# Local and global attention, then two feed-forward layers: another order of TensorE's work in the attention loop

## The chip, the cores and the metric

The kernel runs on one core of a Trainium2 chip. The metric is device time in microseconds (us) of one execution, taken as the median of several runs. A profile is taken of one execution more; its span is the time from the first to the last instruction on the core. The engines work at the same time, each through its own list of instructions in the order in which the program issues them: TensorE (matrix products), VectorE (called DVE in the profile), ScalarE (ACT), GpSimd (POOL). SyncE (SP) issues the transfers between device memory and on-chip memory.

## The reference

Attention has 4 batches and 8 heads, 512 local tokens and 32 global tokens of dimension 64 per head. A global query attends to all 544 keys. A local query attends to the 32 global keys and to the local keys at most 32 positions away. Both results go through two feed-forward layers over 2304 tokens (512 wide, 2048 inside).

```python
def sm(s):
    s = s - np.max(s, axis=-1, keepdims=True)
    e = np.exp(s)
    return e / (np.sum(e, axis=-1, keepdims=True) + 1e-09)
k_all = np.concatenate([k_g, k_l], axis=2); v_all = ...          # the same for values
out_g = sm(scale * q_g @ k_all.T) @ v_all
mask = np.abs(pos[:, None] - pos[None, :]) <= 32
a_l = sm(concat(scale * q_l @ k_g.T, where(mask, scale * q_l @ k_l.T, -1e9)))
out_l = a_l @ concat(v_g, v_l)
x = concat(out_g, out_l)                                          # as (2304, 512)
h = np.maximum(x @ w1_in, 0);  x = (h * h) @ w1_out               # first layer
h = x @ w2_in;  out = (P(h) / (Q(h) + 1e-6)) @ w2_out             # second layer, P and Q polynomials
```

## The kernel before

Heads are worked two at a time: a pair p (16 of them, NP) is two heads on the 128 partitions, 64 each. The 512 local queries of a pair are cut in two units, (p, 0) and (p, 1), of 256 queries. The loop over p runs through 18 iterations; each holds pieces of several pairs, so that an engine always has something of another unit to do while one unit passes from engine to engine.

The pieces of a unit, with the letters that the change's name uses:

- **S**, `scores` (L311): 16 small products of 64x64 tiles into two PSUM banks, `s_ps[0]` and `s_ps[1]` for unit 0, `s_ps[2]` and `s_ps[3]` for unit 1. Each bank belongs to one head (j).
- VectorE's `maxima` (L320, two for each j) add the mask and take the row maximum; ScalarE's `exps` (L328, two for each j) take the exponential and its row sum; VectorE's `sums` and the reciprocal in `norm` (L332, L336) turn the sums round; GpSimd's four `norm` operations (L339) scale the weights.
- **T**, `transp` (L357 and L358): five 128x128 transposes into `tc_ps`. ScalarE copies four of them out (`transp_evac`, L362), VectorE the fifth (L364). GpSimd's `g_copies` (L350) add the weights of the global queries to the same tiles.
- **G**, `glob` in `pv` (L382): the products with the values of the global keys, 128x128 tiles. **W**, `win` (L376): the products with the values of the windows, 128x64 tiles; for unit 1 the last key columns follow (L396, called E here). VectorE copies the result into x (`pv_local` L403, `pv_global` L410 or L412).

The global queries of two pairs (2g and 2g+1) are worked together once every two iterations. **Q**, `g_scores` (L432, 128x64 tiles), writes into two PSUM banks, `s_ps[0]` and `s_ps[1]` (for g = 0 the banks of the value products); VectorE reduces them to a maximum (L435, L436, L441), ScalarE takes two exponentials straight from the banks (`g_exps`, L445, L446), VectorE and GpSimd normalise (`g_norm`, L450 to L452). **X**, `g_transp` (L461, L462), transposes the result into `s_ps[0]` and `s_ps[1]`, and ScalarE copies it out (L464, L465).

The order is written out by hand; no engine's instructions are reordered. In iteration p TensorE has S(p,0), T(p-1,0), G and W of (p-2,1), in odd iterations Q, then S(p,1), in even ones X, then T(p-1,1), G and W of (p-1,0). In the last two iterations, which have no scores, the first products of the feed-forward part (`mm1`) stand in their place.

Beside this the loop converts the first eight weight tiles of the feed-forward part, which arrive as 64-bit floats: ScalarE scales the upper word (`w_scale`, L94), VectorE puts the bits together in three steps (`w_float`, L106, L108, L113) and rounds (`w_split`, L124), GpSimd takes the rest (`w_rest`, L132). The list `slots` says in which iteration each tile is converted, here 6, 8, 10, 14, 16, 16, 17 and 17. In iterations 9 to 12 ScalarE also rounds the first 512 tokens of x (`x_high`, L156), in 10 to 13 VectorE takes their rest (`x_low`, L161). SyncE loads keys and queries of pair p+3 in iteration p, when the buffer of pair p-1 is free, values every second iteration, and weight tiles two iterations ahead of their conversion.

Behind the loop the memory of the attention part is freed, and the feed-forward part runs through steps s of `mm1`, `mm2` and elementwise work, with the other weight tiles loaded and converted on the way.

## Time and profile before

| | |
|---|---|
| time, median of 3 runs | 876.36 us (876.34 to 876.42) |
| the profiled execution | 876.76 us |
| its span | 875.0 us |
| TensorE busy (PE, matrix products) | 864.7 us, 99% of the span |
| VectorE busy (DVE) | 613.7 us, 70% |
| ScalarE busy (ACT) | 549.9 us, 63% |
| GpSimd busy (POOL) | 248.4 us, 28% |
| chain that ended last | PE 92%, DVE 2%, POOL 2%, ACT 1%, issue 1%, DMA 1% |

Busy time is the time in which an engine has at least one instruction under way. TensorE's instructions overlap, so its distance from one start to the next says more than its busy time. A start time in a row is counted from the beginning of the span. A note in brackets behind a row says how long the engine had been idle before and what it waited for.

### The profile page before, as it was taken

What the parts mean: (1) busy time and instruction counts of PE and PEld (TensorE: products, weight loads), DVE (VectorE), ACT (ScalarE), POOL (GpSimd) and SP (SyncE); (2) the same over time, 40 slices, a digit from 0 to 9 for tenths busy, and PEclk for the clock granted to TensorE, in tenths of its full rate; (3) what the DMA queues carried; (4) which work ended last, traced back from release to release, by engine and by line L of the source; (5) the groups of instructions that cost most, each with busy time, mean ns of one, the idle gap of its engine ahead of it and who ended that gap; (6) DMA issues with size and microseconds to landing.
All of it is one profiled execution on the core that took longest, in us unless ns stands there. A gap on an engine that the chain in (4) does not pass through costs nothing.

```text
span 875.0 us, 14523 instructions
## 1 busy us (share of the span) xinstructions
PE 864.7 (99%) x5335; PEld 771.4 (88%) x5335; DVE 613.7 (70%) x1353; ACT 549.9 (63%) x1175; POOL 248.4 (28%) x326
## 2 busy tenths in 40 slices
PE   8999999999999999999999999999999999999998
PEld 4877788888888999999999978888888999999998
DVE  5788888875554576552422599769777987987986
ACT  6888857773333333432445588668666876886885
POOL 4687754440000000000155342212221221221221
PEclk9999999999999999999999999999999999999999
DMA  9686549101553176140044200010001001001001
GB/s 347 261 329 242 212 166 410 75 1 48 169 145 109 46 220 199 47 139 1 25 110 132 73 13 1 0 49 1 1 0 49 1 1 37 1 1 37 1 1 37
DMA packets 27574, 81.67 MB, mean 93 GB/s; under 512 B 3184, under 2 KB 4976, under 8 KB 26480
## 3 DMA queue, kind: packets, MB, share of 16 engines
q1 hardware_dynamic: 27504, 80.76, 27.3%
q8 instruction: 42, 0.69, 0.3%
q14 instruction: 28, 0.23, 0.1%
HBM read 67.90 MB, written 12.85 MB: 92 GB/s over the span
## 4 chain that ended last, share of the span: by engine, by line
PE 92%; DVE 2%; POOL 2%; ACT 1%; issue 1%; DMA 1%; SPq 0%; POOLq 0%; ACTq 0%
PE tc L188 22%; PE pv L188 22%; PE s L175 14%; PE s L177 14%; PE s L176 14%; POOL sm L339 2%; PE pv L376 2%; PE tc L357 2%; PE s L311 1%; PE pv L382 1%; DMA k<-in_kW_dram 1%; PE s L432 1%; DVE sm L320 1%; ACT gs L445 0%; DVE tt L251 0%
## 5 line engine op out<-in xcount | busy, mean ns | idle before, releaser
L175 PE MATMUL s<-xh,w 128*128 128x384 f32 (+1 forms) x640 | 229.7, 359 | 0.0
L177 PE MATMUL s<-xh,w 128*128 128x384 f32 (+1 forms) x640 | 228.4, 357 | 0.0
L176 PE MATMUL s<-xl,w 128*128 128x384 f32 (+1 forms) x640 | 228.2, 357 | 0.0
L260 POOL TENSOR_TENSOR gl<-tt,gh 128x384 fp32r<-128x384 f32 (+1 forms) x79 | 90.1, 1140 | 267.9 <-ACT gh L259 205.2
L188 PE MATMUL tc<-gh,w 128*128 128x384 f32 (+1 forms) x640 | 152.8, 360 | 0.8 <-ACT gh L259 0.8
L188 PE MATMUL pv<-gh,w 128*128 128x384 f32 (+1 forms) x640 | 152.5, 360 | 0.0
L217 ACT ACTIVATE a<-s 128x384 f32<-128x384 f32 (+1 forms) x80 | 42.5, 532 | 152.5 <-PE s L177 152.5
L177 PEld LDWEIGHTS s<-xh,w 128*128 128x128 f32 x640 | 120.1, 188 | 11.4
L176 PEld LDWEIGHTS s<-xl,w 128*128 128x128 f32 x640 | 120.2, 188 | 10.8
L175 PEld LDWEIGHTS s<-xh,w 128*128 128x128 f32 x640 | 120.1, 188 | 10.5
L188 PEld LDWEIGHTS tc<-gh,w 128*128 128x128 f32 x640 | 115.9, 188 | 12.5 <-ACT gh L259 1.7
L188 PEld LDWEIGHTS pv<-gh,w 128*128 128x128 f32 x640 | 115.9, 188 | 11.8
L132 POOL TENSOR_TENSOR w<-raw,w 128x512 fp32r<-128x512 f32 x32 | 42.5, 1347 | 273.1 <-ACT w L126 263.3
L223 DVE TENSOR_TENSOR b<-a 128x384 f32<-128x384 f32 (+1 forms) x64 | 38.3, 599 | 116.2 <-ACT a L217 116.2
L188 PE MATMUL pv<-gl,w 128*128 128x384 f32 (+1 forms) x320 | 89.4, 360 | 0.0
L188 PE MATMUL tc<-gl,w 128*128 128x384 f32 (+1 forms) x320 | 89.2, 359 | 0.0
L237 DVE SCALAR_TENSOR_TENSOR a<-a,nf,b 128x384 f32<-128x384 f32 (+1 forms) x80 | 53.4, 668 | 32.2 <-ACT b L235 32.1
L234 ACT ACTIVATE a<-s 128x384 f32<-128x384 f32 (+1 forms) x80 | 42.0, 525 | 52.7 <-PE s L177 52.7
L339 POOL TENSOR_SCALAR sm<-sm,rs 128x160 f32<-128x160 f32 x128 | 57.1, 471 | 30.3 <-DVE x L410 12.3
L250 DVE SCALAR_TENSOR_TENSOR a<-a,b 128x384 f32<-128x384 f32 (+1 forms) x80 | 49.0, 612 | 22.0 <-ACT b L245 22.0
L188 PEld LDWEIGHTS tc<-gl,w 128*128 128x128 f32 x320 | 58.7, 188 | 6.0
L188 PEld LDWEIGHTS pv<-gl,w 128*128 128x128 f32 x320 | 58.7, 188 | 5.8
(117 smaller groups left out, 1342.4 us busy)
## 6 DMA issues: line engine op xcount, KB each, us to landing
v<-in_v_dram SPq DMA_DIRECT2D x8, 1408.0 KB, 8.3
k<-in_kW_dram SPq DMA_DIRECT2D x15, 592.0 KB, 6.4
r<-in_w1i_dram SPq DMA_DIRECT2D x16, 512.0 KB, 9.5
r<-in_w1o_dram SPq DMA_DIRECT2D x16, 512.0 KB, 10.3
raw<-in_w2i_dram SPq DMA_DIRECT2D x16, 512.0 KB, 4.2
st<-cv SPq DMA_DIRECT2D x32, 256.0 KB, 4.4
raw<-in_w2o_dram SPq DMA_DIRECT2D x16, 512.0 KB, 4.2
raw<-st SPq DMA_DIRECT2D x32, 256.0 KB, 2.7
```

The source lines that it names most:

```text
L132: pool.tensor_tensor(w[:, 1], f, w[:, 0].bitcast(F32), op=ALU.subtract)
L175: pe.matmul(ph, wh, hi[:, kk, :n], start=(kk == 0), stop=False)
L176: pe.matmul(ph, wh, lo[:, kk, :n], start=False, stop=False)
L177: pe.matmul(ph, wl, hi[:, kk, :n], start=False, stop=(kk == KD - 1))
L188: pe.matmul(acc_bank[d][:, :n], w[:, half, 128 * d:128 * d + 128], src[:, :n], start=start, stop=stop)
L217: act.activation(a, ph, AF.Relu)
L223: dve.tensor_tensor(b, a, a, op=ALU.mult)
L234: act.activation(a, ph, AF.Square)
L237: dve.scalar_tensor_tensor(a, in0=a, scalar=nf[:, 5:6], in1=b, op0=ALU.mult, op1=ALU.add)
L250: dve.scalar_tensor_tensor(a, in0=a, scalar=EPS1, in1=b, op0=ALU.add, op1=ALU.mult)
L260: eng.tensor_tensor(gl, t, gh.bitcast(F32), op=ALU.subtract)
L339: pool.tensor_scalar(e, e, rs[:, k:k + 1], 1.0, op0=ALU.mult, op1=ALU.mult)
```

## The change

The pieces stay the same; their order, their lag and a few sizes change. A unit's value products now come an iteration later: in iteration p they are those of b = (p-3, 1) and c = (p-2, 0), and the transposes those of a = (p-1, 0) and d = (p-2, 1). So the loop has one iteration more, and a third `mm1` stands in it. TensorE's list in iteration p is S(p,0), T(a), G(b), in odd iterations Q, W(b), W(c), in even ones X, G(c), T(d), and from iteration 2 on S(p,1) at the end. Maxima and exps of unit (p,1) move to iteration p+1, its normalisation too. The accumulation of a bank begins with G for unit 1 and with W for unit 0. The two reductions of Q move from `g_scores` to `g_scale`, which stands behind the sums of unit (p,0). For the first global scores other places are named: g = 1 is written into `s_ps[2]` and `s_ps[3]`, its exps and transposes stand in iteration 2. The first three weight tiles are converted in iterations 8, 10 and 12 instead of 6, 8 and 10; the first two VectorE steps of a tile stand at the end of its iteration, the third and the rounding at the end of the next one (the last four tiles are done whole). Buffers for values, softmax weights and their transposes grow in number.

```diff
--- before.py
+++ after.py
@@ -264,11 +264,11 @@
     msk_p = att.enter_context(tc.tile_pool(name="msk", bufs=1))
     ident = msk_p.tile([128, 128], F32, name="ident")
     mask = msk_p.tile([128, NB, KW], F32, name="mask")
-    v_p = att.enter_context(tc.tile_pool(name="v", bufs=2))
-    sm_p = att.enter_context(tc.tile_pool(name="sm", bufs=4))
-    pt_p = att.enter_context(tc.tile_pool(name="pt", bufs=3))
+    v_p = att.enter_context(tc.tile_pool(name="v", bufs=3))
+    sm_p = att.enter_context(tc.tile_pool(name="sm", bufs=6))
+    pt_p = att.enter_context(tc.tile_pool(name="pt", bufs=5))
     pg_p = att.enter_context(tc.tile_pool(name="pg", bufs=2))
-    st_p = att.enter_context(tc.tile_pool(name="st", bufs=4))
+    st_p = att.enter_context(tc.tile_pool(name="st", bufs=6))
 
     ff_p = {}
 
@@ -361,35 +361,28 @@
         p1, p2 = pT[p, u]
         act.copy(bass.AP(tensor=p1.tensor, offset=p1.offset, ap=[p1.ap[0], [320, 2], [192, 2], [1, 128]]),
                  tc_ps[0].rearrange("p (a b c) -> p a b c", a=2, b=2))
-        dve.tensor_copy(p2, tc_ps[1][:, 0:128])
-
-    def pv(p, u):
-
-        v = vt[p // 2]
-        c = pgT[p // 2][1]
-        p1, p2 = pT.pop((p, u))
-        bank = pv_ps[u]
-
-        def win(w, o0, o1, stop=False):
+
+    def transp_evac2(p, u):
+        dve.tensor_copy(pT[p, u][1], tc_ps[1][:, 0:128])
+
+
+
+    def pv_glob(p, u):
+        bank, v, p2 = pv_ps[u], vt[p // 2], pT[p, u][1]
+        for i in range(2):
+            o = VG + 256 * (p % 2) + 128 * i
+            pe.matmul(bank[:, 160 * i:160 * i + 128], v[:, o:o + 128], p2, start=bool(u) and i == 0,
+                      stop=not u and i == 1, skip_group_check=True)
+
+    def pv_win(p, u):
+        bank, v, p1 = pv_ps[u], vt[p // 2], pT[p, u][0]
+        for i, (o0, o1) in enumerate(((64, 160), (0, 64), (128, 224), (224, 288))):
             for j in range(2):
-                jj = 2 * (p % 2) + j
-                pe.matmul(bank[64 * j:64 * j + 64, o0:o1], v[:, VW * w + 64 * jj:VW * w + 64 * jj + 64],
-                          p1[:, j, o0 + (32 if o0 >= 128 else 0):o1 + (32 if o0 >= 128 else 0)],
-                          start=False, stop=stop, skip_group_check=True)
-
-        def glob(i):
-            o = VG + 256 * (p % 2) + 128 * i
-            pe.matmul(bank[:, 160 * i:160 * i + 128], v[:, o:o + 128], p2, start=i == 0, stop=False,
-                      skip_group_check=True)
-
-
-        glob(0)
-        glob(1)
-        win(4 * u, 64, 160)
-        win(4 * u + 1, 0, 64)
-        win(4 * u + 2, 128, 224)
-        win(4 * u + 3, 224, 288, stop=u == 0)
+                o, s = VW * (4 * u + i) + 64 * (2 * (p % 2) + j), 32 if o0 >= 128 else 0
+                pe.matmul(bank[64 * j:64 * j + 64, o0:o1], v[:, o:o + 64], p1[:, j, o0 + s:o1 + s],
+                          start=not u and i == 0, stop=False, skip_group_check=True)
         if u:
+            c = pgT[p // 2][1]
             for j in range(2):
                 jj = 2 * (p % 2) + j
                 o = VE + 64 * jj
@@ -418,7 +411,7 @@
     pg2 = [pg_p.tile([128, 128], F32, tag=f"pl{i}", name=f"pl{i}", bufs=1) for i in range(2)]
 
     def g_scores(g):
-        c1, c2 = s_ps[:2] if g else pv_ps
+        c1, c2 = s_ps[:2] if g > 1 else s_ps[2:] if g else pv_ps
         for c in (c1, c2):
             for i in range(2):
                 p = 2 * g + i
@@ -432,12 +425,12 @@
                 pe.matmul(c[o] if c is c1 else c[o, 0:64], qt[p][:, SL:], keys, start=True, stop=True,
                           tile_position=(0, 64 * i))
         m = st_p.tile([128, 8], F32, tag="gm", name="gm")
+        pgs[g] = pg[g % 2], m, c1, c2
+
+    def g_scale(g):
+        s, m, c1, c2 = pgs[g]
         dve.tensor_reduce(m[:, 0:1], c1[:, 32:], axis=AX.X, op=ALU.max)
         dve.tensor_reduce(m[:, 1:2], c2[:, 0:64], axis=AX.X, op=ALU.max)
-        pgs[g] = pg[g % 2], m, c1, c2
-
-    def g_scale(g):
-        s, m, c1, c2 = pgs[g]
         dve.tensor_scalar(m[:, 2:3], m[:, 0:1], m[:, 1:2], -0.125, op0=ALU.max, op1=ALU.mult)
 
     def g_exps(g):
@@ -503,12 +496,12 @@
 
         early = [(0, 0, j) for j in range(N_IN0)] + [(0, 1, j) for j in range(N_OUT0)]
         slots = {}
-        for p, c in zip([6, 8, 10, 14, 16, 16, 17, 17], early):
+        for p, c in zip([8, 10, 12, 14, 16, 16, 17, 17], early):
             slots.setdefault(p, []).append(c)
 
         for k in range(7):
             pe.matmul(pv_ps[0], warm[:, 0:128], warm, start=True, stop=True)
-        for p in range(NP + 2):
+        for p in range(NP + 3):
             if p == NP:
                 open_ff()
             if 1 <= p and p + 3 < NP:
@@ -521,99 +514,122 @@
                 w_load(*c)
             cv = slots.get(p, [])
             cur, pre = p < NP, 1 <= p <= NP
-            odd = p % 2 == 1 and p + 2 < NP
+
+            a = (p - 1, 0) if pre else None
+            b = (p - 3, 1) if 3 <= p else None
+            c = (p - 2, 0) if 2 <= p <= NP + 1 else None
+            d = (p - 2, 1) if 2 <= p <= NP + 1 else None
+            odd, even = p % 2 == 1 and 1 < p < NP - 2, p % 2 == 0 and 0 < p < NP
             g = (p + 1) // 2
 
-            def step(*k):
-                for c in cv:
-                    w_float(*c, k)
+
+            first = cv if p < NP else []
+            whole = cv if p >= NP else []
+            second = slots.get(p - 1, []) if p <= NP else []
 
             if cur:
                 sm_tiles(p, 0)
                 scores(p, 0)
+            elif p - NP < 3:
+                mm1(p - NP)
+            if pre and p > 2:
+                maxima(p - 1, 1, 0)
+                exps(p - 1, 1, 0)
+            if cur:
                 maxima(p, 0, 0)
                 exps(p, 0, 0)
-            else:
-                mm1(p - NP)
-            if 2 <= p:
-                pv_local(p - 2, 0)
-            if pre:
-                sums(p - 1, 1)
+            for n in (a, d):
+                if n:
+                    p_tiles(*n)
+                    if p > 1:
+                        g_copies(*n)
+            if a:
+                transp(*a)
+                transp_evac(*a)
             if cur:
                 maxima(p, 0, 1)
-            if pre:
-                norm(p - 1, 1)
-                p_tiles(p - 1, 0)
-                p_tiles(p - 1, 1)
-                if p > 1:
-                    g_copies(p - 1, 0)
-                    g_copies(p - 1, 1)
-            step(0)
-            if 2 <= p:
-                pv_global(p - 2, 0)
-            step(1)
-            if pre:
-                transp(p - 1, 0)
-                transp_evac(p - 1, 0)
-            step(2)
-            if cur:
                 exps(p, 0, 1)
-            if 2 <= p:
-                pv(p - 2, 1)
-            if odd and p > 1:
+            if p == 1:
+                g_norm(0)
+            if pre and p > 2:
+                maxima(p - 1, 1, 1)
+                exps(p - 1, 1, 1)
+            if a:
+                transp_evac2(*a)
+            if b:
+                pv_glob(*b)
+            if odd:
                 g_scores(g)
-            if cur:
+            if b:
+                pv_win(*b)
+            if c:
+                pv_win(*c)
+            if even and g > 1:
+                g_transp(g)
+            if c:
+                pv_glob(*c)
+            if b:
+                pv_local(*b)
+                pv_global(*b)
+            if d:
+                transp(*d)
+            if p < 2:
                 sm_tiles(p, 1)
                 if p == 0:
                     for k in range(4):
                         pe.matmul(pv_ps[0], warm[:, 0:128], warm, start=True, stop=True)
                 scores(p, 1)
-                if odd and p > 1:
-                    g_scale(g)
-                    g_exps(g)
-                maxima(p, 1, 0)
+                for j in range(2):
+                    maxima(p, 1, j)
+                    exps(p, 1, j)
+            if cur:
                 sums(p, 0)
                 norm(p, 0)
-                exps(p, 1, 0)
-                maxima(p, 1, 1)
-            if p == 1:
-                g_transp(0)
-                g_copies(0, 0)
-                g_copies(0, 1)
-                g_scores(g)
+            if odd or p == 2:
                 g_scale(g)
                 g_exps(g)
-            if odd:
+            if pre:
+                sums(p - 1, 1)
+                norm(p - 1, 1)
+            if c:
+                pv_local(*c)
+                pv_global(*c)
+            if d:
+                transp_evac(*d)
+                transp_evac2(*d)
+            if odd or p == 2:
                 g_norm(g)
-            for c in cv:
-                w_split(*c, dve)
-                w_rest(*c)
-            if p % 2 == 0 and 0 < p < NP:
+            for w in first:
+                w_float(*w, (0, 1))
+            for w in second:
+                w_float(*w, (2,))
+            for w in whole:
+                w_float(*w)
+            for w in second + whole:
+                w_split(*w, dve)
+                w_rest(*w)
+            if p == 2:
                 g_transp(g)
-            if 2 <= p:
-                pv_local(p - 2, 1)
-                pv_global(p - 2, 1)
-            if pre:
-                transp(p - 1, 1)
-                transp_evac(p - 1, 1)
-            if cur:
-                exps(p, 1, 1)
+            if cur and p > 1:
+                sm_tiles(p, 1)
+                scores(p, 1)
             if p == 0:
                 for k in range(4):
                     pe.matmul(pv_ps[0], warm[:, 0:128], warm, start=True, stop=True)
                 g_scores(0)
                 g_scale(0)
                 g_exps(0)
-                g_norm(0)
-            if pre:
-                pv(p - 1, 0)
-            for c in slots.get(p + 1, []):
-                w_scale(*c)
+            if p == 1:
+                g_transp(0)
+                g_copies(*a)
+                g_scores(1)
+            for w in slots.get(p + 1, []):
+                w_scale(*w)
             if 9 < p <= 9 + KD:
                 x_low(0, p - 10)
             if 9 <= p < 9 + KD:
                 x_high(0, p - 9)
-            if p >= NP:
+            if NP <= p:
                 ew1(p - NP)
         att.close()
         act.activation(nf[:, 0:4], cf[:, 0:4], AF.Copy, scale=-1.0)
@@ -644,7 +660,7 @@
         split = []
         made = []
         back = list(reversed(second))
-        used = [1, -1]
+        used = [2, -1]
 
         def load():
 
@@ -696,7 +712,7 @@
 
         load()
         magnitudes(2)
-        for s in range(2, 2 * S1):
+        for s in range(3, 2 * S1):
             t, j = divmod(s, KF)
             mm1(s)
             if j >= LAG:
```

## Rows read from the trace of the kernel before

**Rows 1.** Busy time of each engine by stretch: sum, instructions; then clock, DMA.

```profile
24.70:56.80 32.10, 31.52 (x468) 25.29 (x464) 24.24 (x147) 26.73 (x106) 21.13 (x53) 1.00 0.71 263
56.80:109.20 52.40, 50.62 (x737) 40.64 (x733) 44.22 (x243) 46.53 (x178) 40.57 (x89) 1.00 0.68 255
109.20:123.00 13.80, 13.80 (x117) 11.76 (x115) 10.55 (x27) 7.67 (x17) 7.55 (x10) 1.00 0.13 37
```

**Rows 2.** TensorE's timeline in pairs 11 and 12: start, duration, instruction, count.

```profile
82.72 0.78 PE L376 MATMUL pv<-p,v 128*64 128x96 f32 x16
83.43 0.77 PE L311 MATMUL s<-k,q 64*64 64x160 f32 x16
...
85.80 0.78 PE L376 MATMUL pv<-p,v 128*64 128x96 f32 x16
86.42 0.26 PE L396 MATMUL pv<-pl,v 128*64 128x32 f32 x4
```

**Rows 3.** The chain that ended last, same pairs: start, duration, what.

```profile
88.08 0.48 PE tc L357 x4
...
90.53 0.68 PE tc L357 x4
...
92.56 0.94 PE s L432 x4
```

**Rows 4.** VectorE's timeline in pair 1: start, duration, instruction, idle time before.

```profile
10.48 0.66 DVE L435 TENSOR_REDUCE gm<-pv 128x1 f32<-128x480 f32 x1 [1.93 <-PE pv L432]
...
11.30 0.21 DVE L441 TENSOR_SCALAR gm<-gm 128x1 f32<-128x1 f32 x1
12.69 0.21 DVE L450 TENSOR_SCALAR gm<-gm 128x1 f32<-128x1 f32 x1 [1.18 <-ACT gs L446]
...
13.02 0.31 DVE L320 CUSTOM_DVE_ANT_0 sm<-s,mask 128x160 f32<-128x160 f32 x1
...
15.69 0.21 DVE L332 TENSOR_SCALAR rs<-sum 128x4 f32<-128x4 f32 x1 [0.45 <-ACT sm L328]
15.93 0.18 DVE L336 RECIPROCAL rs<-rs 128x4 f32<-128x4 f32 x1
```

**Rows 5.** ScalarE's timeline in the same stretch.

```profile
11.61 0.66 ACT L445 ACTIVATE gs<-pv,gm 128x480 f32<-128x480 f32 x1 [2.25 <-PE tc L357]
...
12.27 0.30 ACT L446 ACTIVATE gs<-pv,gm 128x64 f32<-128x64 f32 x1
...
13.37 0.44 ACT L328 ACTIVATE sm<-sm,nm 128x160 f32<-128x160 f32 x1 [0.71 <-DVE nm L320]
...
14.23 0.57 ACT L362 COPY p<-tc 128x512 f32<-128x512 f32 x1
14.69 0.45 ACT L328 ACTIVATE sm<-sm,nm 128x160 f32<-128x160 f32 x1
...
16.41 0.56 ACT L464 COPY pg<-pv 128x512 f32<-128x512 f32 x1
```

**Rows 6.** VectorE's groups, pairs 8 to 15: count, busy us, mean ns, idle before.

```profile
L403 DVE COPY x<-pv 128x256 f32<-128x256 f32 x17 | 7.0, 414 | 0.0
...
L161 DVE TENSOR_TENSOR xl<-x,xh 128x512 fp32r<-128x512 f32 x4 | 3.2, 790 | 0.0
...
L108 DVE SCALAR_TENSOR_TENSOR cv<-r,cv 128x512 int32<-128x512 int32 x3 | 2.4, 788 | 0.0
L113 DVE SCALAR_TENSOR_TENSOR cv<-r,cv 128x512 int32<-128x512 int32 x3 | 2.1, 697 | 0.0
...
L124 DVE CAST w<-cv 128x512 fp32r<-128x512 f32 x3 | 1.6, 523 | 0.0
...
L106 DVE TENSOR_SCALAR cv<-cv 128x512 int32<-128x512 int32 x3 | 1.2, 394 | 0.0
```

**Rows 7.** GpSimd's timeline at the turn from pair 7 to pair 8.

```profile
56.18 1.56 POOL L339 TENSOR_SCALAR sm<-sm,rs 128x160 f32<-128x160 f32 x4 [1.04 <-ACT gs L445]
57.71 0.73 POOL L452 TENSOR_SCALAR gs<-gs,gm 128x544 f32<-128x544 f32 x1
```

More of the change, by code (lines that the diff above doesn't have):

```diff
@@ L434, in g_scores @@
         m = st_p.tile([128, 8], F32, tag="gm", name="gm")
-        dve.tensor_reduce(m[:, 0:1], c1[:, 32:], axis=AX.X, op=ALU.max)
-        dve.tensor_reduce(m[:, 1:2], c2[:, 0:64], axis=AX.X, op=ALU.max)
         pgs[g] = pg[g % 2], m, c1, c2
@@ L440, in g_scale @@
         s, m, c1, c2 = pgs[g]
+        dve.tensor_reduce(m[:, 0:1], c1[:, 32:], axis=AX.X, op=ALU.max)
+        dve.tensor_reduce(m[:, 1:2], c2[:, 0:64], axis=AX.X, op=ALU.max)
         dve.tensor_scalar(m[:, 2:3], m[:, 0:1], m[:, 1:2], -0.125, op0=ALU.max, op1=ALU.mult)
```

## The prediction

> **What bounds the kernel now.** I read the page first (TensorE is busy in nearly every slice), then the busy time by stretches [rows 1]. The three stretches are pairs 3 to 7, pairs 8 to 15, and the end of attention up to the fourth matmul group of the feed-forward part. Look there at TensorE against its stretch: 31.52 of 32.10 us, 50.62 of 52.40, 13.80 of 13.80. From 123.00 us to the end of the 875.0 us span the change touches nothing but the moment at which it starts, so I forecast that moment. The other engines are not idle either: in pairs 8 to 15 VectorE has 44.22 and ScalarE 46.53 us of work in 52.40. A pair takes 32.1/5 = 6.42 us in the first stretch and 52.4/8 = 6.55 in the second.
>
> Two views show what TensorE's time is made of. In its timeline, look at distances between starts: W takes 0.71 us when S follows (82.72 to 83.43) and 0.62 when E follows, which keeps the tile shape (85.80 to 86.42) [rows 2]. In the chain of waits T takes 0.68 us behind S and 0.48 behind X, the same shape [rows 3]. So changing the tile shape costs 0.1 to 0.2 us each time. Then I read the lists of VectorE and ScalarE in a stretch without conversions for the delay from one to the other [rows 4, 5]; both run strictly in the written order, and that decides my forecast.
>
> **Fewer changes of shape (gain).** Per pair TensorE now goes S-T-G-W-(E)-S-T-G-W-S: six changes. Afterwards it goes S-T-G-W-E-W-G-T-S-S: four (Q lies beside W and X beside G, free). Removed: two of W to S, at 0.10 on leaving and as I take it 0.05 in the first scores behind, 0.30; one of S to T, 0.20; one of G to W, for which I take 0.14 between the two. Added: W to G, which the trace does not show; I take 0.20 as for entering T, and T to S, 0.15 as for W to S. Net 0.64 - 0.35 = 0.29 us per pair. Each added one could cost from 0 to 0.3, so the net lies between 0 and 0.6 per pair, and only while TensorE is what is waited for.
>
> **Start (loss).** Up to Q of pairs 0 and 1 nothing changes. ScalarE ends their exponentials near 12.6 us [rows 5], and from then its list runs without a gap: a half-unit's two exps take 0.86 (14.69 to 16.41 holds two), a transposed copy 0.46. Up to the accumulated sums of unit (2,0) it has four such pairs and one copy of pair 1 and unit (0,0), the X copies (0.6), another pair, a copy, and a last pair with 1.00 to the VectorE sum (14.69 to 15.69 [rows 4]): 4x0.86 + 0.46 + 0.6 + 0.86 + 0.46 + 1.00 = 6.82, so 19.4 us. Only behind that sum does VectorE now reduce the scores of pairs 2 and 3: sum and reciprocal 0.34, reduce to scale 0.82, to the exp 0.31, between its two parts 0.66, to the norm 0.42, norm 0.33 [rows 4, 5]: 22.3 us. GpSimd meanwhile has two unit norms in its list ahead, 1.56 each from 19.9, so 23.0, then 0.73 for the global norm [rows 7]: 23.7. X of pairs 2 and 3 waits for it, and S(2,1) is written behind X: 0.7 each, so pair 3 starts at 25.1 instead of 24.70 [rows 1]: +0.4. TensorE idles some 3 us before X. What is not done by then (three pieces: two value products and a transposition, 3.3 us) comes back in the extra iteration at the end.
>
> **Iterations (the term that decides).** Let D be how long after the first scores of an iteration VectorE gets free of the last one's list. Its maxima of unit (p-1,1) come first; 0.35 later the exps start (13.02 to 13.37 [rows 4, 5]). ScalarE's order is fixed: pair, pair, copy, pair, and VectorE's sum of unit (p,0) stands behind the third pair: 0.35 + 0.86 + 0.86 + 0.46 + 1.00 = 3.53.
> In an odd iteration the global reduces now stand behind that sum: +0.34 + 0.82 + 0.31 + 0.66 + 0.30 = 5.96. These exps read the two banks that the next S(p+1,0) writes, so S waits: the iteration lasts at least D + 5.9. VectorE is free at 3.53 + 0.34 + 0.82 + 0.31 + 0.66 + 0.42 + 0.33 = D + 6.4.
> In an even iteration S(p+1,0) waits for the copy of X, behind the fourth pair: 0.35 + 4x0.86 + 0.46 + 0.56 = 4.81, at least D + 4.9 with the wait itself. VectorE is free at 3.39 + 1.00 + 0.34 + 0.6 (one 256-column copy, two short ones [rows 6]) = D + 5.35.
> So the excess handed on is 0.5 and 0.45 plus what else stands at the end of VectorE's list, and there the change puts the conversions of the early weights: L106 and L108 in even iterations 8, 10, 12, 14 (0.39 + 0.79, less 0.08 of overlap each as I take it: 1.05 rounded), L113 and L124 in the odd ones behind (0.70 + 0.52: 1.05), and in 10 to 13 the low part of x (0.79: I take 0.65) [rows 6]. Today they stand between waits.
> Without conversions D is about 0.5: TensorE's own work and the waits are about even, pairs 3 to 7 gain 5x0.29 = 1.45 (I let the waits of then and now, some 0.4 in an odd iteration, cancel).
> Pairs 8 to 15: p8 5.8 (TensorE's own work, some 5.6, and 0.2 for a weight scaling ahead of its exps on ScalarE); p9, D = 0.45 + 1.05 = 1.5: 7.4; p10, D = 0.5 + 1.05: 6.45; p11, D = 0.45 + 1.05 + 0.65 = 2.15: 8.05; p12, D = 2.2: 7.1; p13 8.05; p14 7.1; p15 has no Q and no gate: 6.42 - 0.29 - 0.94 [rows 3], 5.1. Sum 55.05 against 52.40: +2.65.
> Each gated iteration also pays semaphore instructions in front of waits; I take 0.1 in each of seven: +0.7 (from 0 to 0.2 each).
>
> **End.** The third feed-forward group now stands inside the attention loop. 13.8 us [rows 1] + 3.3 left from the start - 0.6 of saved changes: 16.5, so +2.7. Weights loaded into freed attention memory get one such group less of lead; the chain L106, L108, L113 (1.7 us at the most after the load [rows 6]) would show as a wait at the sixth group if the cover is gone; I price it at 0. More buffers: 0, memory alone. Keys of a pair are freed at the iteration's end instead of its middle; scores of two iterations later hide that load.
>
> **Sum.** 0.4 - 1.45 + 2.65 + 0.7 + 2.7 = +5.0 us. Against the profiled execution of 876.76 us this is 881.8; against the median of 876.36 it is **881.4 us**.
>
> **A rule that speaks against the change.** Granted clock is 1.00 in every stretch, where TensorE's idle time is 0.58 and 1.78 us in all [rows 1]. The Trainium skill ("TensorE: Matmul & The Clock Gate", "Why this matters for your kernels") warns that a long idle gap between bursts puts the array back to half rate; no row of this trace shows such a fall.
>
> **Rivals.** A, faster: the conversions sink into VectorE's waits, so TensorE stays the bound. Place: pairs 8 to 15; it decides if D stays under about 0.3 in odd and 0.7 in even iterations. Then they lose the 1.78 us of idle time and 8x0.29 = 2.3, -4.1, with no semaphore term: 0.4 - 1.45 - 4.1 + 2.7 = -2.45, 873.9 us. For it: VectorE has 8.2 us without work in that stretch. Against it: the written order, which lets nothing pass a sum that waits.
> B, about the same: iterations 8 to 15 stay as long as now, since VectorE's work is the same in amount: 0.4 - 1.45 + 2.7 = +1.65, 878.0. Against it: the two waits of VectorE per iteration (for the third and the fourth pair of exps) are new in place.
> C, slower still: the 3 us gap before X drops the array from 2.4 to 1.2 GHz, and one iteration's work of 6 us runs twice as long: +6 at the most, 887.4; +2 is nearer, as ScalarE has to be waited for there anyway: 883.4.
> D, the changes of shape cost nothing where the new order has them (the net gain per pair is 0): pairs 3 to 7 lose their 1.45 and the end its 0.6: +7.05, 883.4.
>
> **Chances.** Forecast 0.60, A 0.15, B 0.12, C 0.05, D 0.08. A difference under 0.2% (1.75 us) can't be told from none: faster 0.15, same 0.12, slower 0.73. The range takes in B, A's edge, C's and D's nearer values, and semaphore and shape terms at their ends: 873.5 to 886.0; the forecast's own range is 879 to 884.
>
> **What would show it.** TensorE idle about 3 us up to 23.7 before X (the transposes of the global weights); S(3,0) near 25.1. Then S(p+1,0) behind odd iterations waiting for ScalarE's L445 line, 0.4 us early on and 1 to 2 us from pair 9 to 13, behind even ones for the copy of X; iterations 9 to 14 of 6.4 to 8.1 us. VectorE's first maxima of these iterations begin 1.5 us or more behind the scores they could follow, because conversions run. W and W adjacent at 0.6. The forecast is wrong if S follows S(p,1) without a wait in pairs 9 to 14, or if pair 3 starts well before 25 us.

## The result, and the profile after

The changed kernel takes 884.84 us (median of 4 runs, 884.19 to 885.87) against 876.39 us for the kernel before on the same chip: a ratio of 1.0094, 95% interval 1.0082 to 1.0107, so it is slower by 8.4 us. I had forecast +5.0 us. The time lies outside the forecast's own range of 879 to 884 us; the wide range holds it because that took in the rivals. The profiled execution took 885.87 us with a span of 884.1.

The stretches first, in the view of busy time by stretch: the stretch, its length, then for PE, weight load, DVE, ACT and POOL the busy time and the number of instructions, the granted clock, the DMA share and GB/s. The first row holds the wait in iteration 2 and the start of iteration 3; the other three are pairs 3 to 7, pairs 8 to 15 and the end, which answer to [rows 1].

```profile
20.00:30.00 10.00, 7.07 (x56) 5.43 (x56) 4.25 (x27) 5.25 (x19) 4.22 (x11) 0.66 0.61 233
26.52:59.24 32.72, 32.21 (x472) 25.98 (x464) 23.25 (x144) 26.45 (x106) 17.58 (x48) 0.95 0.66 244
59.24:115.25 56.01, 49.66 (x733) 40.66 (x729) 45.05 (x238) 45.53 (x172) 39.73 (x83) 1.00 0.64 251
115.25:131.65 16.40, 16.40 (x168) 14.38 (x164) 14.30 (x42) 10.92 (x26) 10.49 (x18) 1.00 0.00 1
```

The fourth feed-forward group now starts at 131.65 us in place of 123.00; what follows is as long as before. The 8.65 us split into: start to S(3,0) +1.76 (26.52 against 24.76; how these starts are dated is said with the lengths below), pairs 3 to 7 +0.61 (32.73 against 32.12), pairs 8 to 15 +3.68 (56.00 against 52.32, where TensorE is now without work for 6.35 us), end +2.59 (16.40 against 13.81). The start and pairs 3 to 7 hide something: in the first two rows the clock is not 1.00.

TensorE's timeline of the changed kernel (start, duration, operation, idle time before): the first three rows are the wait in iteration 2 and what follows it, the next five the middle of iteration 3 (they answer to [rows 2, 3]), the last two the gate behind an odd iteration.

```profile
23.75 1.11 PE L454 MATMUL s<-ident,gs 128*128 128x128 f32 x4 [2.94 <-POOL gs L445]
...
25.01 2.41 PE L311 MATMUL s<-k,q 64*64 64x160 f32 x32
27.35 1.13 PE L357 MATMUL tc<-ident,sm 128*128 128x128 f32 x4
...
30.69 0.73 PE L382 MATMUL pv<-p,v 128*64 128x96 f32 x16
31.25 0.26 PE L389 MATMUL pv<-pl,v 128*64 128x32 f32 x4
31.34 0.76 PE L382 MATMUL pv<-p,v 128*64 128x96 f32 x16
32.03 0.71 PE L374 MATMUL pv<-p,v 128*128 128x128 f32 x4
32.58 0.64 PE L357 MATMUL tc<-ident,sm 128*128 128x128 f32 x4
...
45.62 0.77 PE L311 MATMUL s<-k,q 64*64 64x160 f32 x16
46.56 1.06 PE L311 MATMUL s<-k,q 64*64 64x160 f32 x16 [0.16 <-ACT gs L438]
```

X starts at 23.75 behind 2.94 us without work. Then the same instructions take up to 1.8 times as long: four transposes 1.13 us at 27.35 and 0.64 at 32.58. The granted clock is half, 1.2 GHz, from 23.07 to 29.90 us. W now goes to the next product in 0.56 us when E follows and 0.69 when G does.

What X waits for, on VectorE and then on GpSimd (these answer to [rows 4, 7]):

```profile
19.41 0.17 DVE L332 TENSOR_SCALAR rs<-sum 128x4 f32<-128x4 f32 x1 [1.41 <-ACT sm L328]
...
19.70 0.63 DVE L432 TENSOR_REDUCE gm<-s 128x1 f32<-128x480 f32 x1
...
22.07 0.16 DVE L444 RECIPROCAL gm<-gm 128x1 f32<-128x1 f32 x1
```

```profile
19.96 3.05 POOL L339 TENSOR_SCALAR sm<-sm,rs 128x160 f32<-128x160 f32 x8 [0.73 <-DVE rs L336]
22.97 0.72 POOL L445 TENSOR_SCALAR gs<-gs,gm 128x544 f32<-128x544 f32 x1
```

The view of waits for the stretch from 25 to 115 us (who waited for whom: us in all, times, longest) has the two new gates of the scores (L311: behind the exps of L438 in odd iterations, behind the copy of X, L457, in even ones), a third gate that the prediction does not list (Q, L425, behind the maxima that read the banks which Q overwrites), and VectorE's own wait for sums:

```profile
DVE rs L332 <- ACT sm L328: 8.1, 13, 0.9
...
ACT gs L438 <- DVE rs L332: 6.0, 6, 2.3
...
PEld s L425 <- DVE nm L320: 4.9, 8, 1.6
PE s L425 <- DVE nm L320: 3.1, 3, 1.4
PEld s L311 <- ACT gs L438: 2.9, 6, 0.5
PEld s L311 <- ACT pg L457: 2.7, 3, 0.9
```

VectorE's groups in pairs 8 to 15 (count, busy us, mean ns, idle before; they answer to [rows 6]) take no more time than before, the shift L106 apart, 584 ns against 394, but they stand in another place. At the turn to iteration 10 two of them end the list of iteration 9, and the maxima that could have followed the scores of 70.84 us begin at 73.56:

```profile
L108 DVE SCALAR_TENSOR_TENSOR cv<-r,cv 128x512 int32<-128x512 int32 x4 | 3.0, 759 | 0.1
L161 DVE TENSOR_TENSOR xl<-x,xh 128x512 fp32r<-128x512 f32 x4 | 2.7, 676 | 0.0
...
L106 DVE TENSOR_SCALAR cv<-cv 128x512 int32<-128x512 int32 x4 | 2.3, 584 | 0.0
```

```profile
72.39 0.68 DVE L113 SCALAR_TENSOR_TENSOR cv<-r,cv 128x512 int32<-128x512 int32 x1
73.10 0.54 DVE L124 CAST w<-cv 128x512 fp32r<-128x512 f32 x1
73.56 0.31 DVE L320 CUSTOM_DVE_ANT_0 sm<-s,mask 128x160 f32<-128x160 f32 x1
```

The lengths of iterations 3 to 15 on which the rest rests are worked out from the trace, as distances between the last products of S(p,0). A start of S(p,0) is given as that of its last product less 0.43 us, the time from the first product to the last where nothing holds them. Where S is held or at half rate, its first product starts up to 0.4 us earlier than so given (26.13 us for S(3,0) in the changed kernel).

```
            p3    p4    p5    p6    p7    p8    p9    p10   p11   p12   p13   p14   p15
before     6.39  6.17  6.39  6.79  6.38  6.75  6.38  7.08  6.40  6.32  6.39  7.18  5.82
changed    8.03  5.60  6.75  5.60  6.75  5.60  7.28  6.51  8.27  7.10  8.30  7.11  5.83
forecast   -     -     6.4   5.6   6.4   5.8   7.4   6.45  8.05  7.1   8.05  7.1   5.1
```

### The profile page after: what moved, and what is told of

It is laid out like the page before. It is cut to its first block, busy times and chain, and to the rows that moved or that the text cites. A ratio compares the mean times of both kernels' runs of the same rounds, so it can differ in the third digit from the quotient of the medians.

```text
span 884.1 us, 14482 instructions
## 1 busy us (share of the span) xinstructions
PE 866.0 (98%) x5335; PEld 773.3 (87%) x5335; DVE 617.9 (70%) x1353; ACT 549.6 (62%) x1175; POOL 247.1 (28%) x326
## 4 chain that ended last, share of the span: by engine, by line
PE 92%; ACT 3%; DVE 3%; issue 1%; POOL 0%; DVEq 0%; POOLq 0%
PE tc L188 21%; PE pv L188 21%; PE s L175 14%; PE s L177 14%; PE s L176 14%; PE s L311 2%; ACT sm L328 2%; PE tc L357 1%; PE pv L382 1%; PE s L425 1%; PE pv L374 1%; DVE sm L320 0%; DVE tt L251 0%; DVE gm L432 0%; PE pv L503 0%
## 5 line engine op out<-in xcount | busy, mean ns | idle before, releaser
L132 POOL TENSOR_TENSOR w<-raw,w 128x512 fp32r<-128x512 f32 x32 | 42.5, 1347 | 270.1 <-ACT w L126 253.1
L328 ACT ACTIVATE sm<-sm,nm 128x160 f32<-128x160 f32 x128 | 55.2, 439 | 16.9 <-DVE nm L320 16.8
```

The lines of the kernel that those rows point to most:

```text
L132: pool.tensor_tensor(w[:, 1], f, w[:, 0].bitcast(F32), op=ALU.subtract)
L328: act.activation(e, e, AF.Exp, scale=-1.0, bias=nm[:, k:k + 1], accum_out=tot[:, k:k + 1])
```

## The experiments

Theory: iterations are gated by VectorE's written order (lateness is handed on), iteration 3 by half a clock behind X's wait. The rivals are those of the prediction. Each ratio is to the kernel before, run beside it on the same chip; a gain against the changed kernel is the difference of two such ratios.

**e1_fill_gap**: 13 unused matmuls keep TensorE at work in the wait of iteration 2.

```diff
+            if p == 2:
+                for k in range(13):
+                    pe.matmul(pv_ps[1], warm[:, 0:128], warm, start=True, stop=True)
```

> The changed kernel with 13 unused products (0.216 us each at full clock, 2.8 us) put on TensorE into its 2.9 us wait before the second X (g = 1). Theory (the wait lets the clock of the array fall to half, and that is paid again in the next 6.8 us of work): granted clock 1.00 throughout, pair 3 starts near 25.1 instead of 26.65 us, lasts 6.5 instead of 7.85; time 2 to 3 us under that of the changed kernel (884.84): 882 to 883. Rival (the half clock costs nothing, since TensorE waits for the other engines there anyway): 884 to 885 as before, with the clock at 1.00.

Measured: 883.57 us, ratio 1.0076 (1.0061 to 1.0091). In its busy time by stretch and its timeline the clock stays whole, and X and S run at their usual length:

```profile
20.00:30.00 10.00, 9.75 (x113) 6.67 (x113) 5.12 (x32) 6.24 (x24) 4.16 (x11) 1.00 0.60 232
```

```profile
20.40 2.75 PE L578 MATMUL pv<-raw 128*128 128x512 bf16 x12
23.35 0.66 PE L454 MATMUL s<-ident,gs 128*128 128x128 f32 x4 [0.20 <-POOL gs L445]
```

S(3,0) starts at 24.87 and iteration 3 takes 6.77; all later iterations are those of the changed kernel. The fourth feed-forward group starts 2.81 us earlier (128.84 against 131.65). Of this, 0.40 stood ahead of X already (23.35 against 23.75; S(1,0) too starts 0.46 earlier in this execution), so the half clock costs 2.4 us in the profiled execution. By the ratios it is 1.6 us, but their intervals overlap: it is the trace that shows the cost. The stretch at half rate is not equally long in each run, as the next kernel shows. The first product of S(3,0) is at 24.68, 1.33 us behind X; I had forecast 1.4 behind X, at 25.1.

**c_after**: the changed kernel once more.

> The changed kernel once more, for a comparison on the same chip with the runs beside it. Every theory: 1.0094 of the time of before (1.008 to 1.011), half clock somewhere between 22 and 30 us.

Measured: 884.97 us, ratio 1.0094 (1.008 to 1.0108). The half rate lasted 3.4 us here, from 25.2 to 28.6. It began 0.9 us after X had started (24.29, behind 2.94 us without work again). From X to the fourth feed-forward group this execution takes 1.6 us more than that of e1.

**e2_conv_in_waits**: the conversions and x's low part go from the end of VectorE's list to behind the copy of T(a), where VectorE waits for products.

```diff
+            for w in first:
+                w_float(*w, (0, 1))
+            for w in second:
+                w_float(*w, (2,))
+                w_split(*w, dve)
+            if 9 < p <= 9 + KD:
+                x_low(0, p - 10)
...
-            for w in first:
-                w_float(*w, (0, 1))
-            for w in second:
-                w_float(*w, (2,))
```

> The changed kernel with VectorE's conversion steps of the early weights and the low parts of x moved from the end of its list of an iteration to the place behind the copy of T(a), ahead of the sums that wait for ScalarE; the same instructions, the same number. Theory (the end of VectorE's list is handed on to the next iteration's maxima, through exps, sums and the global exps to S(p+1,0)): iterations 9 to 14, now 7.29, 6.51, 8.27, 7.10, 8.30 and 7.11 us, become about 6.5, 5.7, 7.0, 5.7, 7.0, 5.7, and iteration 15 5.1 instead of 5.88: -6 to -7.5 us, 877.5 to 879. Rival B (VectorE's amount of work counts, not its place): 0 to -1 us, 884 to 885.

Measured: 881.22 us, ratio 1.0047 (1.003 to 1.0064), 4.1 us less where 6 to 7.5 were expected. Iterations 9 to 15 are 6.75, 6.09, 7.97, 6.08, 7.97, 5.60, 5.62. The even ones lose 0.4, 1.0 and 1.5 us, where I had said 0.8, 1.4 and 1.4. The odd ones with x's low part hardly move: there the same steps, 2.3 us in iteration 11 (80.59 to 82.91), stand ahead of the reductions instead of ahead of the maxima, and TensorE waits 0.86 us at S where it had waited at Q.

**e3_reduce_first**: the global reductions stand ahead of the copy of b's value product.

```diff
+            if odd or p == 2:
+                g_scale(g)
             if b:
                 pv_local(*b)
...
             if odd or p == 2:
-                g_scale(g)
                 g_exps(g)
```

> The changed kernel with VectorE's reductions of the global scores ahead of the copy and the sums of unit (p,0), not behind. Theory (the sum that waits for the third pair of exps holds the reductions back, so that the global exps end 0.7 us later than ScalarE's own order needs): odd iterations 3 to 13 each lose about 0.65 us (5 and 7: from 6.75 to 6.1), together -3.3 to -4.2 us: 880.6 to 881.5. Rival (the odd iterations are held by ScalarE's amount of work or by GpSimd, the sum's place is no matter): 0 to -0.5 us.

Measured: 881.03 us, ratio 1.0049 (1.0034 to 1.0064), 3.9 us less, as expected: odd iterations 6.07, 6.07, 6.91, 7.58, 7.56. With the gate's wait away a clean odd iteration is 6.07 us, in which TensorE works without a gap. In the kernel before, iteration 3 took 6.39, without a gap as well.

**e4_start_as_before**: the second global unit's reductions, exponentials and norm stand in iteration 1 again.

```diff
-            if odd or p == 2:
+            if odd:
                 g_scale(g)
                 g_exps(g)
...
             if p == 1:
...
+                g_scale(1)
+                g_exps(1)
+                g_norm(1)
```

> The changed kernel with maximum, exps and norm of the second global scores (g = 1) in iteration 1 directly behind the scores, as the kernel before has them. Theory (X of g = 1 and with it pair 3 wait for this chain): TensorE's wait before that X goes from 2.9 us to under 1, the clock stays at 1.00, S(3,0) starts near 22.7 instead of 26.65; in all -4 us against 884.84 (2.3 of the wait, some 1.7 of clock): 880.5 to 881.5. Rival (the start is limited by ScalarE's and GpSimd's amount of work, so the time is lost a few iterations later): within 1 us of the result of filling the gap, 882 to 883.

Measured: 882.21 us, ratio 1.006 (1.0045 to 1.0075), 3.0 us less where about 4 were expected. No half clock, S(3,0) at 23.00. But iteration 3 takes 7.45: Q of pairs 4 and 5 is now ready before its keys. The waits between 24 and 27.5 us, and the load of those keys (issued at 13.77 us; last number: us to landing) in the view of DMA:

```profile
PEld s L425 <- DMA k<-in_kW_dram: 0.5, 1, 0.5
```

```profile
k<-in_kW_dram SPq DMA_DIRECT2D x1, 592.0 KB, 11.8
```

**e5_delay_vector**: two unused 128x512 VectorE operations end the lists of iterations 4 and 6.

```diff
+            if p in (4, 6):
+                flat = mask.rearrange("p a b -> p (a b)")
+                for _ in range(2):
+                    dve.tensor_tensor(idle, flat[:, 0:512], flat[:, 128:640], op=ALU.max)
```

> The changed kernel with two unused VectorE operations (128x512, about 0.6 us each, 1.2 together) at the end of VectorE's list of iterations 4 and 6, which hold no conversion. Theory (what stands at the end of that list is handed on): iterations 5 and 7, now 6.75, become D + 5.9 with D = 0.45 + 1.2, so 7.4 to 7.6; 4 and 6 stay at 5.60, and 6 and 8 may take up to 0.2 more; +1.3 to +1.9 us in all. Rival B (VectorE has spare time, some 2.5 us in each iteration, in which 1.2 us vanishes): iterations 5 and 7 stay at 6.75, time as that of the changed kernel.

Measured: 886.1 us, ratio 1.0111 (1.0097 to 1.0124). Iterations 5 and 7 go from 6.75 to 7.72 and 7.73, the even ones stay at 5.60. In its timeline the two operations take 1.72 us:

```profile
40.46 1.72 DVE L630 TENSOR_TENSOR idle<-mask 128x512 f32<-128x512 f32 x2
42.11 0.31 DVE L321 CUSTOM_DVE_ANT_0 sm<-s,mask 128x160 f32<-128x160 f32 x1
```

The maxima start at 42.11 in place of 40.47, 1.64 later; Q waits 0.81 us for them, and 0.97 of the 1.64 reach the next scores. (By the ratios the kernel is 1.5 us slower, with overlapping intervals; the rows show it.) Lateness is handed on; rival B (only the amount of VectorE's work counts) would have had it sink into the 9.5 us that VectorE has without work in pairs 3 to 7 (32.72 less 23.25).

**e6_all**: e2, e3 and e4 together, with x's low part between the two units' norms.

> The changed kernel with three repairs: the second global scores' maximum, exps and norm in iteration 1 as in the kernel before; the global reductions ahead of the copy and the sums; conversions behind the copy of T(a), the low parts of x between the norms of the two units. Theory: odd iterations 6.1 to 6.4, even 5.6 to 5.8, iteration 3 up to 6.8 since the scores of pairs 4 and 5 wait for their keys; S(3,0) near 23: 11 us under e4, 870 to 872, 0.7% under the kernel before. Rival (ScalarE is the next bound: its work in iterations 9 to 12 alone is 24.2 us against 23.3 of TensorE, and it gives back what the repairs save): 873 to 877. Rival B (amount of VectorE's work): as e4, 881 to 882.

Measured: 877.46 us, ratio 1.0008 (0.9999 to 1.0017), as fast as before but not the 870 to 872 expected, nor the rival's 873 to 877. Iterations 4 to 10 are near what I had said (5.60, 6.07, 5.60, 6.07, 5.60, 6.19, 6.08); iteration 11 takes 9.48 and 13 takes 7.76. The cause stands in VectorE's timeline ahead of iteration 11, with GpSimd's beside it:

```profile
67.70 2.66 DVE L106 TENSOR_SCALAR cv<-cv 128x512 int32<-128x512 int32 x1
70.39 0.69 DVE L108 SCALAR_TENSOR_TENSOR cv<-r,cv 128x512 int32<-128x512 int32 x1
```

```profile
67.63 0.74 POOL L445 TENSOR_SCALAR gs<-gs,gm 128x544 f32<-128x544 f32 x1
68.31 1.30 POOL L132 TENSOR_TENSOR w<-cv,w 128x512 fp32r<-128x512 f32 x1
69.53 0.55 POOL L350 COPY p<-pg 128x128 f32<-128x128 f32 x2
```

The shift L106, 0.40 us in the kernel before [rows 6], is held for 2.3 us and ends just behind GpSimd's run. T(a) of iteration 11 then waits 1.01 us, and the clock is half for 3.4 us from 73.9.

**e7_more_shapes**: e6 with G(c) ahead of W(c), two changes of tile shape more per iteration (six in place of four).

```diff
+                pv_glob(*c)
             if c:
                 pv_win(*c)
...
-            if c:
-                pv_glob(*c)
```

> As e6, but G(c) ahead of W(c), so that W(b) and W(c) are no more adjacent: per iteration one change from W to G and one from G to W are added and G to T becomes W to T or W to X. Same instructions. Theory (a change of tile shape costs 0.1 to 0.2 us on TensorE, and TensorE is the bound in e6): +0.34 us per iteration, 13 to 16 of them, +4 to +5.5 us over e6. Rival D (the changes cost nothing, since another engine is waited for): within 1 us of e6.

Measured: 879.05 us, ratio 1.0026 (1.0017 to 1.0035). Clean iterations take 5.92 and 6.40 against 5.60 and 6.07: 0.32 and 0.33 us for the two, so rival D (changes of shape cost nothing) falls. The total gives 1.6 us between the medians where 4 to 5.5 were expected: iterations 9 to 14 are held by other engines, and the profiled execution of e6 has a stretch at half rate that this one has not. I have not traced the rest.

**e8_conv_idle and e9_conv_idle_x**: in e8 the shift and the cast stand in odd iterations, the or-steps in even ones; e9 also takes x's split in iterations 4 to 7.

```diff
-            for w in first:
-                w_float(*w, (0, 1))
-            for w in second:
-                w_float(*w, (2,))
-                w_split(*w, dve)
+            for w in slots.get(p + 1, []) if p + 1 < NP else []:
+                w_float(*w, (0,))
+            for w in first:
+                w_float(*w, (1, 2))
+            for w in second:
+                w_split(*w, dve)
...
-            if 9 < p <= 9 + KD:
-                x_low(0, p - 10)
+            if 3 < p <= 3 + KD:
+                x_low(0, p - 4)
```

> The kernel of e6_all with the four steps of a weight conversion spread over three iterations: the shift (the int32 operation on one SBUF tensor, 0.40 us alone) one iteration earlier, in the odd one, and with it there the cast of the chunk before (L124), both in the place where GpSimd waits for its reciprocals; the two or-steps (L108, L113) in the even iteration. Loads and scalings are one iteration earlier too. Theory (the shift was held in e6_all until GpSimd's list was empty, 2.66, 2.31 and 2.15 us, and that is where iterations 11 and 13 went, 9.48 and 7.76 us): each shift takes 0.40 to 0.6 us, iterations 9, 11, 13 take 6.2 to 7.2, iterations 10 and 12 5.9 to 6.2, the chain reaches the fourth product of the next stage at 119 to 121 us in place of 123.5, and the time is 871 to 875. Rival (VectorE's amount of work in these iterations is what held e6_all, wherever the steps stand): iterations 9 to 13 sum to 36 to 37.5 as they did there (37.3 without that kernel's half clock) and the time stays at 876.5 to 878.5.

> The kernel of e8_conv_idle with the four steps that split the attention's result for the next stage (ScalarE's copy and VectorE's subtraction of 0.66 us) in iterations 4 to 7 in place of 10 to 13, where no conversion stands. Theory (in iterations with neither conversion nor split VectorE has slack, in those with both it has none): iterations 4 to 7 are longer by 0 to 0.2 us each, iterations 10 to 13 shorter by 0.3 to 0.6 each, 0.8 to 1.6 us less in all than e8_conv_idle: 870 to 874. Rival (the subtractions lie beside waits in both places): within 0.5 us of e8_conv_idle.

Measured: 877.85 us, ratio 1.001 (1.0001 to 1.0019), and 877.31 us, 1.0001 (0.9993 to 1.001). Both missed: the shift now takes 0.74 to 1.09, but the first operation in the old place, now L108, is held in its stead (2.92 us in e8, 2.86 in e9, in iteration 10). Moving x's split brought 0.5 us between the medians, about what the rival allows.

**e10_shift_places**: the changed kernel with an unused shift of the same form in two places, beside GpSimd's norms (iteration 4) and beside an idle GpSimd (iteration 6).

```diff
+            if p == 6:
+                dve.tensor_scalar(idle, idle, 3, None, op0=ALU.logical_shift_left)
...
+            if p == 4:
+                dve.tensor_scalar(idle, idle, 3, None, op0=ALU.logical_shift_left)
```

> The changed kernel with the same unused operation (an int32 shift of a 128x512 SBUF tensor into itself) in two places: at the end of VectorE's list of iteration 4, where GpSimd is at its norms, and behind the copy of the first unit's transposes in iteration 6, where GpSimd waits. Theory (the shift is held until GpSimd has nothing to do): 1.8 to 2.4 us in the first place, ending as GpSimd's norms and copies end, and iteration 5 longer by 1.2 to 1.9 us; 0.40 to 0.45 us in the second, and iteration 6 unchanged at 5.60 or up to 0.2 longer. Rival (a shift costs what it takes alone wherever it stands, and in e6_all it waited for its input): 0.40 to 0.45 in both, iteration 5 longer by 0.4 at most. Time 886 to 887.5 by the theory, 884.9 to 885.5 by the rival.

Measured: 884.16 us, ratio 1.0081 (1.0065 to 1.0096). The theory that a shift waits until GpSimd has nothing to do falls: beside a run of eight norms it took 0.66 us, beside nothing 0.42. The rival's 0.40 to 0.45 in both places is missed by this too, though iteration 5 stays at 6.75. The time lies below both ranges.

```profile
39.05 0.66 DVE L631 TENSOR_SCALAR idle<-idle 128x512 int32<-128x512 int32 x1
...
48.27 0.42 DVE L562 TENSOR_SCALAR idle<-idle 128x512 int32<-128x512 int32 x1
```

```profile
37.86 3.27 POOL L340 TENSOR_SCALAR sm<-sm,rs 128x160 f32<-128x160 f32 x8 [2.16 <-DVE rs L337]
```

**e11_low_vector**: e9 with the weights' low parts (L132) on VectorE, in the even iteration.

```diff
+            for w in slots.get(p - 2, []) if p <= NP else []:
+                w_rest(*w, dve)
...
-            for w in second + whole:
+            for w in whole:
                 w_rest(*w)
```

> The kernel of e9_conv_idle_x with the low parts of the four weight chunks (L132, 1.28 us on GpSimd) taken by VectorE, one iteration later, behind the or-steps of the even iteration (0.67 us estimated from L161, the same form and size). In e9_conv_idle_x the or-step L108 took 2.86 and 2.85 us in iterations 10 and 12 with L132 starting 0.56 us behind it, and 0.92 to 1.33 elsewhere. Theory (it is the run of GpSimd work with L132 in it that holds VectorE's operation, since beside GpSimd's norms alone a shift took 0.66 us): without L132 each L108 takes 0.7 to 1.4 us, iterations 11 and 13 6.4 to 7.0 in place of 8.10 and 8.08, even iterations up to 6.3, iterations 8 to 15 49.5 to 50.8 us in place of 51.4, the fourth product of the next stage at 120 to 121.5 us in place of 121.6, and the time 875 to 877. Rival (VectorE's operation waits for the end of whatever run GpSimd is in): L108 in iterations 10 and 12 shorter only by L132's own time, 1.5 to 2.2 us, the 0.67 us on VectorE comes on top, iterations 11 and 13 at 7.4 to 8.1, and the time 877 to 878.5.

Measured: **874.54 us** (873.87 to 875.38), ratio 0.9975 (0.9964 to 0.9985): faster than both kernels, by 2.2 and 10.3 us, and lower than either expectation. VectorE's and GpSimd's timelines ahead of iteration 11:

```profile
68.92 1.60 DVE L108 SCALAR_TENSOR_TENSOR cv<-r,cv 128x512 int32<-128x512 int32 x1
70.55 0.69 DVE L113 SCALAR_TENSOR_TENSOR cv<-r,cv 128x512 int32<-128x512 int32 x1
71.16 0.69 DVE L132 TENSOR_TENSOR w<-cv,w 128x512 fp32r<-128x512 f32 x1
```

```profile
68.76 0.74 POOL L445 TENSOR_SCALAR gs<-gs,gm 128x544 f32<-128x544 f32 x1
69.43 0.55 POOL L350 COPY p<-pg 128x128 f32<-128x128 f32 x2
```

L108 is shorter by 1.26 us, the time of L132 (1.28), and iterations 11 and 13 take 7.42 in place of 8.10 and 8.08. On the mechanism that is the rival's forecast: L108 still ends only behind GpSimd's run of L445 and L350. On the total neither was right: the profiled executions of e9 and e11 differ by only 0.7 us at the fourth feed-forward group (121.62 and 120.94; 876.16 and 875.38 us as a whole), but e9's runs spread from 875.12 to 878.54, and what its longer ones hold no trace shows. Against the kernel before the profile gains 2.06 us: start -1.98 (S(3,0) at 22.78), iteration 3 +1.47, iterations 4 to 15 -4.14 (73.91 against 78.05), end +2.59 (16.40). No run undoes the longer end; its price is read from rows alone.

## Why the prediction was right, and what its size missed

The direction held, and so did the mechanism in the main: VectorE's lateness is handed on as waits of TensorE. The +5.0 us came out as +8.45. A term that I had left out of the sum, the clock, cost about 2.4 us; pairs 3 to 7 gained 0.8 less than I had put; and in the odd iterations the chain ran over instructions that I had not listed.

- Start. X at 23.75 behind 2.94 us without work (forecast 23.7 and some 3 us). With the clock kept whole (e1) S(3,0) followed X by 1.33 us (forecast 1.4). Right.
- The clock. This is the step that failed, rival C, to which I gave 0.05 because no row of the kernel before showed a fall. It costs 2.4 us in the profiled execution, 1.6 by the ratios; my nearer value for it, +2, was about right, its chance was not. The rule that I had quoted is that of the Trainium skill ("TensorE: Matmul & The Clock Gate", "Why this matters for your kernels"): a long idle gap puts the array back to half rate. The trace after agrees with it, 1.2 GHz from 23.07 to 29.90 us, and by it the forecast would have been that of C, 883.4. How long the wait was does not decide alone: in e6 half rate follows a wait of 1.01 us, while the changed kernel keeps a clock of 1.00 behind the waits of 1.36 and 1.37 us in iterations 11 and 13.
- Changes of shape. W to G costs 0.13 on leaving (0.69 against 0.56 to E), where I took 0.20; two changes more per iteration cost 0.32 in e7, where I had taken 0.29 for the two saved, and an odd iteration without a gap takes 6.07 (e3) against 6.39 before, 0.32 less. Right. The mean of 5.60 and 6.75, 6.18, is near the 6.13 forecast only because it holds 0.68 of a new wait (6.75 less 6.07); that is luck.
- Odd iterations without conversions, 6.75 where I had 6.4. The step omitted: on VectorE the copy of b's value product stands ahead of the sum and waits for E:

```profile
43.92 0.42 DVE L396 COPY x<-pv 128x256 f32<-128x256 f32 x1 [1.16 <-PE pv L389]
44.27 0.18 DVE L405 TENSOR_TENSOR x<-x,pv 128x32 f32<-128x32 f32 x1
44.36 0.16 DVE L332 TENSOR_SCALAR rs<-sum 128x4 f32<-128x4 f32 x1
```

  S(5,0) is at 40.14 and the maxima start 0.33 later; my list puts the sum 3.53 behind that, at 44.00. It is at 44.36, and that is the 0.35. (e3 takes the reductions out of this place.) With the clock whole (e1) pairs 3 to 7 take 31.46 us, 0.66 less than before, where I had 1.45 less: the waits of then and now, which I had let cancel, do not.
- Iterations 8 to 14: 5.60, 7.28, 6.51, 8.27, 7.10, 8.30, 7.11 against 5.8, 7.4, 6.45, 8.05, 7.1, 8.05, 7.1. In length the carry rule, "D of the conversions", is right to 0.25 us, and e5 shows that lateness is carried. In the odd iterations it took another path. I had S wait 1 to 2 us for the global exps in pairs 9 to 13; ahead of its first product it waits 0.16 to 0.20 us for them, with conversions and without. TensorE waits at Q instead, 0.38, 1.36 and 1.37 us in iterations 9, 11 and 13, for the maxima. From Q the chain goes over W and E to the copy of b's value product and only then to the sum. The chain that ended last, in iteration 11:

```profile
81.65 0.23 DVE sm L320
...
81.95 1.20 PE s L425 x6
...
83.15 0.56 PE pv L382 x12
...
83.90 0.42 DVE x L396
```

  My list led over ScalarE's third pair of exps instead. Both paths are about equally long, so that the lengths came out all the same; that is luck. In the even iterations 10, 12 and 14 the next S does wait for the copy of X, by 0.54 to 0.62 us. The separate term of 0.7 for semaphores is not seen apart: without it the forecast for pairs 8 to 15 is 2.65, with it 3.35, and 3.68 came.
- Iteration 15, 5.83 in place of 5.1: T(d) waits 0.39 us for ScalarE's copy of T(a), a wait that I had not listed. The other 0.34 is in what I started from: I took 6.42 less 0.94, 5.48, for an iteration without Q, and in the kernel before iteration 15 takes 5.82. (My terms also give 5.19 and not 5.1.)
- End: 16.40 (forecast 16.5).

Taken together, the profile's 8.65 us less 2.4 for the clock are 6.25, against 5.0. The rivals: A asked that the conversions sink into waits, which they do only in part when moved there (e2: 4.1 us of the 6 to 7.5 expected). B falls with e2, where the same work of VectorE in other places takes 4.1 us less, and with e5. D falls with e3 and e7.

## What to carry to other kernels

When two in-order engines hand work back and forth, write out both lists up to the instruction that frees the next bank, with every copy that stands in them and for every product that writes a bank (Q as well as S); what ends the list late is handed on, whatever slack the busy time shows. Behind a new wait on TensorE half rate can follow (here 3.4 or 6.8 us of it behind a wait of 2.94 us, 3.4 behind one of 1.01); give it a price and a chance of its own. Where operations are moved on VectorE, look at what GpSimd is doing at that moment: the same operation cost between 0.4 and 2.7 us by its place.

## What the hardware showed that I had not expected

Some of VectorE's operations between tensors in SBUF, the on-chip memory, were held by GpSimd's. L108 takes 0.70 to 0.79 us in the kernels before and after; it took 1.60 against a run of L445 and L350 and 2.86 to 2.92 with L132 in that run, ending 0.3 to 0.6 us behind it; L106 took 2.66 in place of 0.40. The Trainium skill ("SBUF — State Buffer", "Who interferes with whom") says that VectorE and GpSimd share a pair of ports, for which a VectorE instruction contends when it has two inputs in SBUF or runs in a 2-port mode (one that uses this pair beside its own), and that in such a mode whichever issues first has the pair for its whole instruction while the other is blocked. That fits the direction; no trace shows in which mode L106, which has one input, ran. The traces go beyond the rule, since VectorE was held over three to four GpSimd instructions in a row, yet a shift beside a run of norms was held for 0.24 us only. What makes the norms let it in and the other run not stays open: form, size and order differ together, and no run separates them.
